# A long convolution and a two-layer block on one core: first x chunk in two loads of 96 rows, its second cast behind two tiles, fewer fillers, last-stage pieces of batch 0 in pairs

## The chip, the cores and the metric

The kernel runs on one core of one Trainium2 chip. The time is device microseconds of that core, from the kernel's start to its end. The profile is one execution of the program, taken by the hardware profiler. Engines: PE is TensorE (matmul; PEld its weight loads), DVE is VectorE, ACT is ScalarE, POOL is GpSimd, SP is SyncE, which here only issues transfers.

## The reference

```python
X = np.fft.rfft(x, axis=1)                      # x: 8 batches, 3008 positions, 256 channels
Y = X * (filt_r + 1j * filt_i)[None, :, :]
y = np.fft.irfft(Y, n=3008, axis=1)
h = y.reshape(24064, 256) @ w_in                # 256 x 2048
s = np.sin(alpha * h)
g = h + s * s / (alpha + 1e-09)
out = g @ w_out                                 # 2048 x 256
```

All inputs and the output are float32; inside, the kernel computes in float16 with float32 accumulation.

## The kernel before

**The transform.** 3008 is 47 x 64, so the transform of each channel is done in four stages of small matrix products per batch: stage 1 over the 47, stage 2 over the 64 with the twiddles in its table (`d_t`), the product with the filter, the inverse of stage 2 (`e_t`), and the last stage (`wi_t`), whose result is written to `y`, which has room for two batches. x is read as 94 rows (`NR`) of 32 x 256 values: row r holds positions 32r to 32r + 31.

**Batch 0 (the head)** has code of its own and stays on the chip between stages, because nothing else can run beside it. Its x is loaded in four chunks. Chunk 0 comes over the hardware queues in float32 into `x32` (lent by `cos_all`): for each half, 80 rows are issued on SP and 14 on ACT, and the table `wf0_t` is issued on ACT between the two. Chunks 1 to 3 are cast on the way by POOL's queue (`load_x`), behind which POOL issues `d_t`, the identity `id16`, the filters and `e_t`. VectorE casts chunk 0 in two halves; then come 16 products of stage 1 (`pa`, L364), evacuated by VectorE (even) and ACT (odd) into `t1_0`. VectorE turns `t1_0` by 32 x 32 blocks (`turn`), copies each filter half to the other partitions (`other_half`), and multiplies (`product_0`). TensorE makes the tables `e1_0` by transposing `d_t` (`pse`, L340), does stage 2 (`pb`, L393) and its inverse (`pc`, L412, through the pool `fps` of two PSUM buffers, evacuated by ACT), and after `turn_back` the last stage.

**Fillers.** `warm_pe(n)` issues n matmuls on zeros (L351) whose result nobody reads, in places where TensorE would stand idle: 19 before stage 1, 2 between groups of stage 1, 5 after it, and 2 and 4 around the first last-stage pieces.

**The last stage** comes in 16 pieces per batch: `last(u)` takes four columns of 94 and one half of the channels. For batch 0 a piece is eight matmuls of 64 columns (`pd`, L258), a buffer of `fps`, and an evacuation into `y`. Without an argument `evac` gives one in three to VectorE and two to ACT, by a counter.

**The dense block** runs over 48 chunks of up to 512 columns of `y`, two batches at a time, in 8 steps each: `hidden` (`ph`, L497, four `hps` buffers; sine on ACT, L500; L501 on VectorE into `v`) twice per step, and `project` of the chunk before (`po`, L513) between. All spectral work of batches 1 to 7, and pieces 4 to 15 of batch 0, is put between dense groups by a list with due times in steps (`put(at, fn, ...)`): `slot(at)` takes what is due, at most one TensorE item at a time unless it is late by more than a step.

```python
for u in range(4, 16):
    put((1,2,3,4,5,6,7,9,16,18,20,22)[u - 4], s0.last, u, pe=True)
...
put(7.5 + 0.3 * i if b == 1 else ..., s.first, i, pe=True)
...
put(12.5 if b == 1 else max(z - 56, 46.5), s.load_t2, g)
```

So batch 1's stage 1 (`first`, `pa`, L183) is due in steps 7.5 to 12; its tiles go to DRAM over SP (`d<-t_h`), come back turned over POOL's queue (`t<-d`, `load_t2`), and its stage 2 (`forward`, `pb`, L203) is due from step 17.5 on. Each engine runs its instructions in the order written; the order in the program is the order of the queues.

Of the kernel before, what the change touches and what calls it, by code (L numbers as in the profile page):

```python
# [18 lines left out]
B, S, C = 8, 3008, 256  # L19
# [3 lines left out]
NR = 2 * N1  # L23
# [39 lines left out]
def kernel(  # L63
# [10 lines left out]
    nc = tc.nc  # L74
# [4 lines left out]
    wf0_dram = nc.inline_tensor(wf0_host, name="wf0_tbl")  # L79
# [38 lines left out]
    cos_all = cpool.tile([128, 4, 512], FP32)  # L118
    y = cpool.tile([128, 2, 2, 32, NR], FP16)
    y_cols = y.rearrange("p a b n r -> p a (b n r)")  # L120
    alpha = y_cols[:, :, 32 * NR:32 * NR + DFF].bitcast(FP32)
    x32 = cos_all.rearrange("p a b -> p (a b)")[0:NR]
    wf0_t = cpool.tile([96, 128], FP16)
    for h in range(2):
        for q, (r0, r1) in ((nc.sync, (0, 80)), (nc.scalar, (80, NR))):
            q.dma_start(out=x32[r0:r1, 4 * C * h:4 * C * h + 4 * C],
                        in_=bass.AP(tensor=x.tensor, offset=x.offset + (32 * r0 + 4 * h) * C,
                                    ap=[[32 * C, r1 - r0], [1, 4 * C]]))
        if h == 0:
            nc.scalar.dma_start(out=wf0_t, in_=wf0_dram.ap())  # L130
    d_t = cpool.tile([128, NS, 128], FP16)
    e_t = cpool.tile([128, NS, 128], FP16)
    wi_t = cpool.tile([NK, NR], FP16)
# [6 lines left out]
    def load_x(b, ch):  # L140
        xt = xpool.tile([NR, 8, C], FP16, name=f"x_{b}_{ch}", tag="x")
        for n0, n in [(0, 8)] if b or ch < 3 else [(0, 4), (4, 4)]:
            ins = nc.gpsimd.dma_start(  # L143
                out=xt[:, n0:n0 + n],
                in_=bass.AP(tensor=x.tensor, offset=x.offset + (b * S + ch * 8 + n0) * C,
                            ap=[[32 * C, NR], [C, n], [1, C]]),
            )
        if b == 0:
            marks["x", ch] = ins
        if b == 1:  # L150
            marks["x1", ch] = ins
            after(ins, marks["w_out"])
        if b > 1:
            after(ins, marks["snake"])
        return xt
# [3 lines left out]
    def evac(dst, src, on_act=None):  # L159
        flip[0] = (flip[0] + 1) % 3  # L160
        if flip[0] if on_act is None else on_act:
            marks["act"] = nc.scalar.copy(out=dst, in_=src)  # L162
        else:
            marks["dve"] = nc.vector.tensor_copy(out=dst, in_=src)  # L164

    class Spectral:
# [82 lines left out]
        def last(self, u, on_act=None):  # L249
# [12 lines left out]
                                     lhsT=t4_h[ch // 2][0:NK, n0 % 16 + i, cb * 128:cb * 128 + 128])  # L262
            evac(y[:, cb, self.b % 2, n0:n0 + 4, :], psv, on_act)

    warm = cpool.tile([128, 1], FP32)
    nc.vector.memset(warm, 0.0)
    nc.scalar.activation(out=warm, in_=warm, func=AFT.Sin)
# [6 lines left out]
    x0 = [xpool.tile([NR, 8, C], FP16, name="x_0_0", tag="x")] + [load_x(0, ch) for ch in range(1, 4)]  # L274
# [17 lines left out]
    def spread_alpha(i):  # L292

        ps = hps.tile([128, 4, 128], FP32, name=f"al_bc_{i}", tag="h")
        for a in range(4):
            for k, part in enumerate(parts):
                nc.tensor.matmul(out=ps[:, a, :], lhsT=one[:, 4 * i + a:4 * i + a + 1].to_broadcast([16, 128]),
                                 rhs=part, start=(k == 0), stop=(k == 2))
        nc.scalar.copy(out=alpha[:, i // 2, 512 * (i % 2):512 * (i % 2) + 512], in_=ps.rearrange("p a b -> p (a b)"))

    for g in range(2):
        gs = slice(12 * g, 12 * g + 12)
        for k, filt in enumerate((filt_r, filt_i)):
            for q in range(2):
                if (g, k, q) == (0, 1, 1):
# [3 lines left out]
                    out=f_t[k][64 * k + 32 * q:64 * k + 32 * q + 32, gs, :],  # L309
                    in_=bass.AP(tensor=filt.tensor, offset=filt.offset + off,  # L310
                                ap=[[N1 * C, 32], [step, 12], [1, C]]))
# [34 lines left out]
    def warm_pe(n):  # L346

        warmed.append(n)
        ps = hps.tile([128, 512], FP32, name=f"warm_{len(warmed)}", tag="h")
        for i in range(n):  # L350
            nc.tensor.matmul(out=ps, lhsT=idle[:, 0:128], rhs=idle[:, 0:512], start=True, stop=True)  # L351
# [3 lines left out]
        gs = slice(12 * g, 12 * g + 12)  # L355
        evac(f_t[k][64 - 64 * k:128 - 64 * k, gs, :], f_t[k][64 * k:64 * k + 64, gs, :], on_act)

    warm_pe(19)
    for h in range(2):
        evac(x0[0].rearrange("p n c -> p (n c)")[:, 4 * C * h:4 * C * h + 4 * C], x32[:, 4 * C * h:4 * C * h + 4 * C], False)  # L360
    for i in range(16):
        own, tag = (fps, "f") if i % 3 == 2 else (hps, "h")
        ps = own.tile([128, 512], FP32, name=f"pa_0_{i}", tag=tag)
        nc.tensor.matmul(out=ps, lhsT=wf0_t[0:NR], rhs=x0[i // 4][:, 2 * (i % 4):2 * (i % 4) + 2, :],  # L364
                         start=True, stop=True)
        evac(t1_0[:, 2 * i:2 * i + 2], ps.rearrange("p (n c k) -> p n c k", n=2, k=2), i % 2)
        if i < 15 and i % 4 == 3:
            warm_pe((2, 2, 2, 5)[i // 4])
    spread_alpha(0)
    spread_alpha(1)  # L370
    warm_pe((2, 2, 2, 5)[3])

    def turn(dst, src):

# [69 lines left out]
    s0 = Spectral(0)  # L444
# [32 lines left out]
    warm_pe(2)  # L477
    s0.last(0, True)
    s0.last(2, True)
    warm_pe(4)  # L480
    s0.last(1, True)
    s0.last(3, False)

# [62 lines left out]
    def put(at, fn, *args, pe=False):  # L546
        pending.append((at, len(pending), pe, fn, args))
# [9 lines left out]

    for i in range(2):
        put(13 + i, negate, i)
    for u in range(4, 16):  # L560
        put((1,2,3,4,5,6,7,9,16,18,20,22)[u - 4], s0.last, u, pe=True)
    for b in range(1, B):
        s = s1 if b == 1 else Spectral(b)
        z = 48 * b
# [87 lines left out]
```

## Time and profile before

| | us |
|---|---|
| four runs | 794.33, 794.27, 794.33, 793.78 |
| median | 794.3 |
| profiled execution, whole | 793.05 |
| its span, first to last instruction | 791.3 |
| PE busy in the span | 779.0 |
| DVE, ACT, POOL busy | 656.5, 617.4, 77.5 |

TensorE is busy for 98% of the span; a busy time here includes the fillers. Most lines of the profile name the program's line, the engine, and what is written and read (`pd<-wi_t,t_h`); a wait is put down to what came last. The head reaches to about 38 us, where the first dense group starts; batch 0's pieces 4 to 11 run from 39.6 to 56, and batch 1's stage 1 from 50 to 65.

### The profile page before, as it was taken

Reading aid. Unit: us, or ns where it says so; the run is one execution under the profiler, and the core shown is the slowest. Engines: PE = TensorE matmul, PEld = TensorE weight load, DVE = VectorE, ACT = ScalarE, POOL = GpSimd, SP = SyncE. Lnnn points to the kernel's source line nnn. Section 1 sums busy time; section 2 is a strip of 40 time slices with the busy share of each in tenths; the row PEclk is TensorE's granted clock in tenths of the full one; section 3 lists DMA queues with packets and bytes.
Section 4 is the critical chain, followed back from the end, with each engine's and each line's share of the span. In section 5 each row is a group of like instructions: output and inputs, shape, how many; then the busy total and the mean of one; then the engine's idle time right before and its main releaser. Section 6 shows DMA issues by size and latency. Waiting matters only on the chain.

```text
span 791.3 us, 16750 instructions
## 1 busy us (share of the span) xinstructions
PE 779.0 (98%) x5865; PEld 536.8 (68%) x5865; DVE 656.5 (83%) x1170; ACT 617.4 (78%) x1210; POOL 77.5 (10%) x119
## 2 busy tenths in 40 slices
PE   8999999999999999999999999999999999999997
PEld 4755666666667766776666766777666776766665
DVE  6877897799878997799978998799987999777773
ACT  5886887888878888788787888788887887777663
POOL 5442000200020000200020000200002000000000
PEclk9999999999999999999999999999999999999999
DMA  9956477755573646654475454845566243421111
GB/s 214 256 107 165 102 157 194 185 108 131 140 204 83 123 111 182 159 117 110 111 209 128 101 107 136 222 90 114 127 169 166 63 99 80 116 60 28 40 41 54
DMA packets 87677, 100.99 MB, mean 128 GB/s; under 512 B 14476, under 2 KB 75932, under 8 KB 87592
## 3 DMA queue, kind: packets, MB, share of 16 engines
q1 hardware_dynamic: 78024, 73.62, 34.3%
q0 software_dynamic: 9296, 26.13, 17.6%
q8 instruction: 46, 0.75, 0.4%
q14 instruction: 39, 0.32, 0.1%
q10 hardware_dynamic: 272, 0.17, 0.1%
HBM read 55.70 MB, written 46.66 MB: 129 GB/s over the span
## 4 chain that ended last, share of the span: by engine, by line
PE 93%; ACT 2%; DMA 2%; DVE 1%; issue 1%; ACTq 0%; POOL 0%; POOLq 0%; DVEq 0%
PE po L513 40%; PE ph L497 39%; PE pa L183 3%; PE pb L203 2%; PE pd L261 2%; PE pc L234 2%; PE pd L258 1%; DVE v L501 1%; ACT cos_all L500 1%; DMA cos_all<-in_x_dram 1%; PE pb L393 1%; PE warm L351 1%; ACT t_h L162 1%; PE pc L412 1%; DMA t<-d 0%
## 5 line engine op out<-in xcount | busy, mean ns | idle before, releaser
L501 DVE SCALAR_TENSOR_TENSOR v<-cos_all,ph 128x512 f16<-128x512 f32 (+1 forms) x768 | 483.0, 671 | 111.7 <-ACT cos_all L500 108.4
L500 ACT ACTIVATE cos_all<-ph 128x512 f32<-128x512 f32 (+1 forms) x768 | 410.9, 591 | 98.6 <-PE ph L497 97.2
L513 PE MATMUL po<-w,v 128*128 128x256 f16 x3008 | 388.7, 272 | 0.0
L497 PE MATMUL ph<-y,w 128*128 128x512 f16 (+1 forms) x1536 | 386.8, 374 | 1.0 <-ACT y L162 0.7
L513 PEld LDWEIGHTS <-v 128*128 128x128 f16 x3008 | 289.3, 98 | 78.2 <-issue 1.8
L497 PEld LDWEIGHTS <-w 128*128 128x128 f16 x1536 | 147.3, 98 | 104.0 <-issue 2.4
L519 ACT COPY o<-po 128x512 f32<-128x512 f32 (+1 forms) x97 | 55.7, 575 | 19.6 <-PE po L513 13.7
L206 ACT CAST xf<-pb 128x512 f16<-128x512 f32 x84 | 49.9, 594 | 16.2 <-PE pb L203 14.1
L195 POOL DMA_DIRECT2D t<-d x56 | 36.3, 667 | 204.8 <-DMA out_dram<-o 129.9
L162 ACT CAST t_h<-pa 96x512 f16<-96x512 f32 x77 | 44.9, 585 | 9.9 <-PE pa L183 9.8
L143 POOL DMA_DIRECT2D x<-in_x_dram x32 | 17.1, 538 | 300.3 <-PE pc L234 160.4
L162 ACT CAST y<-pd 128x376 f16<-128x376 f32 x83 | 39.8, 480 | 7.5 <-PE pd L261 5.3
L261 PEld LDWEIGHTS <-t_h 96*128 96x128 f16 x448 | 31.3, 97 | 18.7 <-DMA t_h<-d 0.6
L183 PE MATMUL pa<-x,wf_t 94*96 94x512 f16 x112 | 42.3, 381 | 1.2 <-DVE t_h L164 0.6
L162 ACT CAST g<-pc 128x512 f16<-128x512 f32 x56 | 33.3, 594 | 7.5 <-PE pc L234 7.2
L224 DVE TENSOR_TENSOR p<-p,xs 128x512 f16<-128x512 f16 x84 | 35.7, 425 | 2.9
L261 PE MATMUL pd<-wi_t,t_h 96*128 96x94 f16 x448 | 37.1, 204 | 0.2 <-ACT cos_all L500 0.2
L223 DVE TENSOR_TENSOR xs<-xs,filt_t 128x512 f16<-128x512 f16 x84 | 35.0, 417 | 0.3 <-DMA xs<-xf 0.3
L217 DVE TENSOR_TENSOR p<-xf,filt_t 128x512 f16<-128x512 f16 x84 | 35.0, 417 | 0.0
L203 PE MATMUL pb<-t,d_t 128*128 128x256 f16 x168 | 32.1, 272 | 1.1 <-DMA t<-d 1.0
L234 PE MATMUL pc<-p,e_t 128*128 128x256 f16 x168 | 32.1, 273 | 0.0
L164 DVE CAST y<-pd 128x376 f16<-128x376 f32 x45 | 24.4, 542 | 0.6 <-PE pd L258 0.5
(63 smaller groups left out, 259.4 us busy)
## 6 DMA issues: line engine op xcount, KB each, us to landing
x<-in_x_dram POOLq DMA_DIRECT2D x30, 376.0 KB, 4.9
d<-t_h SPq DMA_DIRECT2D x28, 384.0 KB
t<-d POOLq DMA_DIRECT2D x56, 192.0 KB, 4.8
xs<-xf SPq DMA_DIRECT2D x168, 64.0 KB
d<-g SPq DMA_DIRECT2D x56, 192.0 KB
t_h<-d SPq DMA_DIRECT2D x28, 384.0 KB
out_dram<-o SPq DMA_DIRECT2D x104, 80.0 KB
w_out<-in_moe_w_out_dram SPq DMA_DIRECT2D x1, 2048.0 KB
```

What stands on the lines that cost most here:

```text
L162: marks["act"] = nc.scalar.copy(out=dst, in_=src)
L183: marks["pe"] = nc.tensor.matmul(out=ps[0:NK, :], lhsT=wf_t, rhs=self.x[ch][:, 2 * j:2 * j + 2, :], start=True, stop=True)
L195: nc.gpsimd.dma_start(out=self.t2[g][64 * p:64 * p + 64, :, :], in_=self.d1[a0:a0 + 6, :, :].rearrange("s n c -> n s c"))
L203: nc.tensor.matmul(out=ps[:, i, :], lhsT=d_t[:, s, :], rhs=self.t2[s // 6][:, s % 6, :], start=True, stop=True)
L206: nc.scalar.copy(out=self.xf[u], in_=ps)
L234: nc.tensor.matmul(out=ps[:, i, :], lhsT=e_t[:, 2 * w + i, :], rhs=pt[:, i, :], start=(k == 0), stop=(k == len(pr) - 1))
L261: nc.tensor.matmul(out=psv[:, i, :], rhs=wi_t, start=True, stop=True, lhsT=t4_h[ch // 2][0:NK, n0 % 16 + i, cb * 128:cb * 128 + 128])
L497: nc.tensor.matmul(out=ps[:, 0:n], lhsT=w1[:, cb, jb * 128:jb * 128 + 128], rhs=y_cols[:, cb, c0:c0 + n], start=(cb == 0), stop=(cb == 1))
L500: nc.scalar.activation(out=cs[:, 0:n], in_=ps[:, 0:n], func=AFT.Sin, bias=float(np.pi / 2))
L501: marks["snake"] = nc.vector.scalar_tensor_tensor(out=v[k][:, jb, 0:n], in0=cs[:, 0:n], scalar=-1.0, in1=ps[:, 0:n], op0=ALU.add, op1=ALU. ...
L513: nc.tensor.matmul(out=pso[k][:, t % 2, :], lhsT=v[k][:, jb, 128 * t:128 * t + 128], rhs=w2[:, jb, :], start=(jb == 0), stop=(jb == 15))
L519: nc.scalar.copy(out=o[:, i0:t % 2 + 1, :], in_=pso[k][:, i0:t % 2 + 1, :])
```

## The change

Chunk 0 of x is loaded by two transfers on SP of 96 rows each; the two rows beyond 94 hold values of the next batch and are not read afterwards. The table `wf0_t` becomes the first transfer that ACT issues. The second cast of chunk 0 is written behind stage 1's tiles 0 and 1, with three fillers ahead of it on TensorE. The filler counts change as shown. Pieces 4 to 15 of batch 0 are put as six pairs; of a pair, the first is evacuated by ACT and the second by VectorE. On TensorE the order after batch 1's stage 2 has begun is the same but for the pieces that have been moved ahead: pieces 4 to 11 stand ahead of batch 1's stage 1, 12 to 15 between its stage 1 and its stage 2, where before 11 stood inside its stage 1 and 13, 14 and 15 behind the start of its stage 2.

```diff
-    x32 = cos_all.rearrange("p a b -> p (a b)")[0:NR]
+    x32 = cos_all.rearrange("p a b -> p (a b)")[0:96]
     wf0_t = cpool.tile([96, 128], FP16)
     for h in range(2):
-        for q, (r0, r1) in ((nc.sync, (0, 80)), (nc.scalar, (80, NR))):
-            q.dma_start(out=x32[r0:r1, 4 * C * h:4 * C * h + 4 * C],
-                        in_=bass.AP(tensor=x.tensor, offset=x.offset + (32 * r0 + 4 * h) * C,
-                                    ap=[[32 * C, r1 - r0], [1, 4 * C]]))
-        if h == 0:
-            nc.scalar.dma_start(out=wf0_t, in_=wf0_dram.ap())
+        nc.sync.dma_start(out=x32[:, 4 * C * h:4 * C * h + 4 * C],
+                          in_=bass.AP(tensor=x.tensor, offset=x.offset + 4 * h * C, ap=[[32 * C, 96], [1, 4 * C]]))
+    nc.scalar.dma_start(out=wf0_t, in_=wf0_dram.ap())
...
+        def last_two(self, u):
+            self.last(u, True)
+            self.last(u + 1, False)
...
-    warm_pe(19)
-    for h in range(2):
-        evac(x0[0].rearrange("p n c -> p (n c)")[:, 4 * C * h:4 * C * h + 4 * C], x32[:, 4 * C * h:4 * C * h + 4 * C], False)
+    warm_pe(10)
+    def cast_x0(h):
+
+        cs = slice(4 * C * h, 4 * C * h + 4 * C)
+        evac(x0[0].rearrange("p n c -> p (n c)")[:, cs], x32[0:NR, cs], False)
+
+    cast_x0(0)
     for i in range(16):
...
+        if i == 1:
+            warm_pe(3)
+            cast_x0(1)
         if i < 15 and i % 4 == 3:
-            warm_pe((2, 2, 2, 5)[i // 4])
+            warm_pe((2, 2, 2, 1)[i // 4])
     spread_alpha(0)
     spread_alpha(1)
-    warm_pe((2, 2, 2, 5)[3])
+    warm_pe((2, 2, 2, 1)[3])
...
-    warm_pe(4)
+    warm_pe(1)
     s0.last(1, True)
     s0.last(3, False)
...
-    for u in range(4, 16):
-        put((1,2,3,4,5,6,7,9,16,18,20,22)[u - 4], s0.last, u, pe=True)
+    for u in range(4, 16, 2):
+        put((1,2.5,4,6,14,16)[u // 2 - 2], s0.last_two, u, pe=True)
```

## The prediction

> **What bounds the kernel now.** I read the page first, then TensorE's waits, then the chain that ended last, stage by stage, and beside it the timeline of VectorE in the head.
>
> ```profile
> span 791.3 us, 16750 instructions
> PE 779.0 (98%) x5865; PEld 536.8 (68%) x5865; DVE 656.5 (83%) x1170; ACT 617.4 (78%) x1210; POOL 77.5 (10%) x119
> PEclk9999999999999999999999999999999999999999
> ```
>
> TensorE is busy for all but 12 us of the span, at full clock. So an edit pays in two ways only: less time on TensorE, or one of its few waits gone. The waits (who waited for whom, total, times, longest):
>
> ```profile
> PE pa L364 <- DVE x L164: 1.1, 1, 1.1
> PE pb L203 <- DMA t<-d: 1.0, 1, 1.0
> ...
> PE pa L183 <- DVE t_h L164: 0.6, 1, 0.6
> ```
>
> The first is in the head, which the change rebuilds; the second is near 75 us, between batch 1's stage 1 and its stage 2. The chain in the head (start, length, what):
>
> ```profile
> 1.78 6.31 DMA cos_all<-in_x_dram
> ...
> 8.18 0.70 DVE x L164
> ...
> 8.93 0.59 PE pa L364 x2
> ...
> 14.85 1.19 PE warm L351 x5
> 16.04 1.01 PE pse L340 x32
> ```
>
> The first x chunk's second half holds everything: its 14-row load, third on ACT's queue, lands at 8.1. But TensorE is not what carries the head on from there. VectorE's timeline is:
>
> ```profile
> 8.79 5.30 DVE L164 CAST t<-pa 128x512 f16<-128x512 f32 x8
> 14.26 2.37 DVE L375 STREAM_TRANSPOSE t_h<-t 128x1024 uint32<-128x1024 uint32 x2 [0.17 <-ACT t L162]
> 24.21 0.95 DVE L164 COPY filt_t<-filt_t 64x3072 f16<-64x3072 f16 x1
> 25.31 2.97 SPq L427 DMA_DIRECT2D w_in<-in_moe_w_in_dram  x6
> 25.92 0.96 DVE L164 COPY filt_t<-filt_t 64x3072 f16<-64x3072 f16 x1
> ```
>
> Eight evacuations end to end, then transposes, copies and products with hardly a gap until 31 us. The w_in loads at 25.31 wait for the last filter load, so that line shows when it lands: the copy at 25.92 can come at most 0.6 earlier. Later in the chain:
>
> ```profile
> 33.87 1.08 PE pd L258 x16
> 35.92 1.15 PE pd L258 x16
> 41.25 0.66 PE pd L258 x8
> 41.91 0.97 PE ph L497 x4
> 66.57 3.28 DMA d<-t_h
> 71.12 3.62 DMA t<-d
> 75.25 0.86 PE ph L497 x4
> 76.11 0.61 PE pd L258 x8
> 76.72 0.98 PE po L513 x8
> ```
>
> A last-stage piece (8 narrow matmuls) costs 0.61 to 0.66 alone; two in a row cost 1.08 to 1.15. The dense group behind a piece takes 0.97 or 0.98, where it takes 0.86 or 0.87 elsewhere.
>
> **The change part by part.**
>
> *Loads of x.* Two SP loads of 96 rows replace two of 80 on SP and two of 14 on ACT; ACT loses two issues (0.66 and 0.43 us), so the wf load is issued at about 0.75 and not 1.43. Rows 94 and 95 add 2%. By the trace's landing records the two SP halves land near 4.95 and 6.4, the wf table at 6.7, ACT's second half at 8.1. For the 96-row half I bound the landing by 6.4 (the 80-row row, nothing added) and 8.1 (nothing gained). [...] By the rows, what was late was one small load behind two others on its own queue, while SP's own half was there 1.7 sooner; a fifth more rows on SP adds a few tenths. I take 7.0, the nearer row. The later issues of POOL are untouched, and the DMA row of the page stands at 9 or more through the head, so the x chunks 1 to 3, tables and filters land as before.
>
> *Second cast behind two tiles.* VectorE now takes tile 0's evacuation (0.66) ahead of the cast (0.70). First cast 5.2 to 5.9, tiles 0 and 1 at 6.0 (before 7.25, where the 19 fillers ended), evacuation to 7.1, second cast to 7.8, tile 2 at 7.85 instead of 8.93: 1.1 earlier. Queued behind the cast are all other evacuations on VectorE. With x chunk 1 landing at 8.5 and the last piece of chunk 3 at 11.8 (issue near 3.0 plus the 8.8 that the trace gives), the last tile runs at 11.9, stage 1 is evacuated at 13.2 and not 14.23, and the transposes start 1.0 earlier.
>
> Then the stall moves. The identity table lands at 15.1 (issue 4.03 plus 11.1), so the `pse` transposes gain 0.8 at most of the 16.04. The copies of the filters at 24.21 and 25.92 meet their loads: gain 0.5 there. From 28 on TensorE and ACT alternate through two PSUM buffers (the evacuation of each `pc` ahead of the next but one), and ACT, 0.75 ahead by then, brings that chain forward by 0.7. Ends for the head are 0.2 (the filter copies rule, and a bit more is lost) and 1.0 (stage 1's whole gain is kept); I take **0.7**.
>
> *Fillers.* 19 become 10 plus 3; 5 and 4 become 1 each. Eight run at half rate (0.43 us) and end at 4.9, so ten end at 5.3, then 0.7 idle. Where TensorE waits for VectorE anyway they cost nothing; their loss costs something only through the clock. [...] By the trace the price is 0: a gap of 1.08 and a 3.4 us stretch (7.05 to 10.45) with only 2.32 busy kept clock 1.00. The longest new idle is 1.3 (13.9 to 15.2). [...] I take 0.
>
> *Pairs.* Twelve single pieces of batch 0 become six pairs, one evacuated by ACT, one by VectorE; that is nearly the split of before. A single with what it adds to the group behind costs 0.65 + 0.11 = 0.76 among the first eight (0.62 + 0.11 = 0.73 among the last four); a pair 1.11 + 0.11 = 1.22. Early: 8 x 0.76 - 4 x 1.22 = 1.2. Late: 4 x 0.73 - 2 x 1.22 = 0.5. But from 45.7 to 51 the chain runs over ACT (sines, four w_out scalings, evacuations), whose work stays the same. So chunk 0 ends about where it did, with piece 11 done inside it; what stays is that piece's absence from chunk 1, and of 1.2 I take **0.7** (0 to 1.2). Late: **0.5**. Each pair fills both stage PSUM buffers, so the next stage 1 tile waits for ACT's and VectorE's copy in queue order; two dense groups lie between, and I add nothing.
>
> *Where the late pairs stand.* Pieces 13, 14 and 15 used to come after `pb_0`, the product that waits 1.0 us for batch 1's reload; now all stand ahead of it. The write and reload (66.57 to 74.74) start from batch 1's last stage 1 tile, and TensorE's work from there to `pb_0` grows from 8.7 by 2 x 1.22 - 0.73 = 1.7, against a path of 9.5. The wait is covered with 0.9 to spare: **1.0**.
>
> Sum: 0.7 + 0.7 + 0.5 + 1.0 = 2.9. The profiled execution took 793.05 (span 791.3 and 1.75 around it), 1.25 below the median of the four runs; it would take 790.2. The same 2.9 off the median of 794.3 gives 791.4. After 75 us the orders are the same and TensorE is busy throughout, so I see nothing that gives the gain back; I round to 791.5.
>
> **The rivals.**
>
> *Covered gains.* The 96-row half lands near 8, or the filter copies hold the head, and ACT takes all of the early pairs' gain. Only the covered reload and the late pairs are left: 1.0 + 0.5, so 792.8. For it: the ACT stretch of the chain; DMA engines full in the head. Against: SP's own half at 6.4.
>
> *The clock gate closes in the head, and it ends slower.* The place is 5.3 to 15.2, with idle stretches of 0.7, 0.7 and 1.3 us and few fillers. TensorE at half rate costs about 0.5 us for each us of its work on the path: sixteen tiles 3.4 more, the alpha spread 1.4, `pse` and `pb` 2.4, together 7.2, of which idle time takes 2.5. So 4.7 is lost against 2.9 won: 796.1. It decides from about 6 us at half clock. Against: the 3.4 us stretches of before that are only two thirds busy at full clock.
>
> *The change does less than it says:* tile 0's evacuation holds the second cast past the time that its data is there. With the landing at 6.4 this costs 0.7 of a gain that the filter copies cap anyway; it is inside the range of the forecast.
>
> **How the numbers follow.** A change of 0.2% (1.6 us) is about what a measurement of this kernel can tell from none: faster is below 792.7, slower above 795.9. Forecast 0.64 (its own range 790.2 to 792.7), covered gains 0.20 (792.2 to 794.3, a quarter of it below 792.7), clock 0.10, something unlisted on the slow side 0.03, more gain than summed (chunk 1's waits of 0.6 and 0.4 going too) 0.03. Faster 0.64 + 0.05 + 0.03, less a little for the forecast's edge: 0.70; same 0.17; slower 0.13. The range runs from 790.2 to 794.3; it leaves out the clock case and about 0.05 below.
>
> **What would show it.** Right: tile 2 (`pa`, third) near 7.85; stage 1's last evacuation near 13.2; `ph_0` 0.7 earlier than 36.98; pairs as groups of 16 at 1.1; no wait of `pb` on the reload; PEclk still 9 everywhere. Wrong: a clock digit below 9 in the first slices; the second cast waiting for its load until 8; a wait of stage 1 on an evacuation where pairs hold the buffers; or a new wait after 80 us as long as the one removed.

## The result, and the profile after

| | median us (executions) | ratio to the kernel before, 95% interval |
|---|---|---|
| before | 794.33 (50) | 1 |
| changed | 793.28 (32) | 0.9988 (0.9983 to 0.9993) |

The change makes the kernel 0.12% faster: more than the interval, less than the 0.2% that the prediction called a difference, and a third of the 2.9 us that the sum gave. The profiled execution took 793.69 us. From its page:

```profile
span 791.9 us, 16719 instructions
...
PEclk9899999999999999999999999999999999999999
```

The 8 in the last line is new: in the second slice (20 to 40 us) TensorE was not at full clock. A shorter closing of the clock in the first slice, shown below, does not change its digit: with 3.41 us of 19.8 at half clock the mean is still 0.91. TensorE's waits now:

```profile
PE pse L341 <- DMA id<-id: 1.0, 1, 1.0
PE pd L258 <- DMA t_h<-d: 0.8, 1, 0.8
...
PE pa L369 <- DVE x L161: 0.5, 1, 0.5
```

The wait of `pb` on its reload is gone, as forecast, and so is half of the first one. But `pd` of batch 1 now waits for a transfer, where before only its weight load did, for 0.6:

```profile
PEld L261 <- DMA t_h<-d: 0.6, 1, 0.6
```

The chain shows both losses:

```profile
38.85 1.82 PE ph L505 x4
40.67 1.16 PE pd L255 x16
...
67.93 1.11 PE pd L255 x13
...
76.43 0.22 PE pb L200 x2
...
122.29 4.85 DMA d<-g
...
127.21 3.94 DMA t_h<-d
...
131.20 0.34 PE pd L258 x4
```

Four hidden products take 1.82 at 38.85, where they took 0.97: half clock. The pairs are there at 1.1 each, and `pb` (76.43) no longer waits. At 131 the first last-stage piece of batch 1 waits for its write and reload.

To see where the gain is won and lost, I compare the start of the same matmul in both traces. From `pb_4` on the orders are equal, so matmuls can be matched from the end:

| place (time before) | changed is ahead by, us |
|---|---|
| first hidden product (36.98) | 0.52 |
| third hidden product (38.6) | -0.18 |
| batch 1's first stage 1 tile (49.9) | -2.19 (with piece 11 already done) |
| 88.5 | 0.77 |
| 127 | 0.43 |
| 131.5, and then constant to 785 | -0.18 |

After 131 us the matmuls of the two traces run in step to 0.02 us: on TensorE everything is decided before. What comes behind the start of the last matmul took 5.79 us and not 5.34; over all traces here it takes 5.0 to 6.0. This execution is 0.4 over the changed kernel's median, and that of the kernel before, with which every trace below is compared too, is 1.3 under its own (793.05 against 794.33). So a gain read from two traces can be smaller than the one that the medians show, and what the kernel before did in its one trace need not be its rule.

### The profile page after: what moved, and what is told of

The parts are those of the page before. It is cut to its first block, busy times and chain, and to the rows that moved or that the text cites. A ratio compares the mean times of both kernels' runs of the same rounds, so it can differ in the third digit from the quotient of the medians.

```text
span 791.9 us, 16719 instructions
## 1 busy us (share of the span) xinstructions
PE 778.0 (98%) x5852; PEld 536.8 (68%) x5852; DVE 657.7 (83%) x1171; ACT 616.9 (78%) x1209; POOL 78.1 (10%) x119
## 4 chain that ended last, share of the span: by engine, by line
PE 89%; DMA 3%; DVE 3%; ACT 2%; issue 1%; SPq 0%; POOL 0%; ACTq 0%; POOLq 0%
PE ph L505 39%; PE po L521 39%; PE pa L180 3%; PE pd L258 2%; PE pb L200 2%; PE pc L231 2%; DVE v L509 1%; DMA id<-id 1%; PE pd L255 1%; ACT cos_all L508 1%; DMA xs<-xf 1%; DMA d<-g 1%; PE pb L401 1%; DVE t_h L383 1%; ACT t_h L159 1%
## 5 line engine op out<-in xcount | busy, mean ns | idle before, releaser
L203 ACT CAST xf<-pb 128x512 f16<-128x512 f32 x84 | 49.9, 594 | 15.1 <-PE pb L200 12.7
L180 PE MATMUL pa<-x,wf_t 94*96 94x512 f16 x112 | 42.2, 381 | 1.1 <-DVE t_h L161 0.6
L159 ACT CAST g<-pc 128x512 f16<-128x512 f32 x56 | 33.3, 594 | 7.5 <-PE pc L231 7.2
```

What stands on the lines that cost most here:

```text
L180: marks["pe"] = nc.tensor.matmul(out=ps[0:NK, :], lhsT=wf_t, rhs=self.x[ch][:, 2 * j:2 * j + 2, :], start=True, stop=True)
L203: nc.scalar.copy(out=self.xf[u], in_=ps)
```

## The experiments

**The two groups of fillers.** The clock by stretches of 3.41 us in the changed kernel (columns: stretch, its length, busy us and count of PE, PEld, DVE, ACT and POOL, granted clock, DMA share, GB/s), set where the trace's clock record changes:

```profile
11.46:14.88 3.42, 2.42 (x28) 1.66 (x28) 3.15 (x4) 2.48 (x4) 0.90 (x2) 1.00 1.19 261
14.88:18.29 3.41, 3.24 (x44) 2.90 (x43) 3.11 (x4) 2.14 (x3) 2.62 (x4) 0.50 1.17 221
...
25.12:28.53 3.41, 2.64 (x37) 2.21 (x35) 3.28 (x5) 3.41 (x8) 0.00 (x0) 1.00 0.72 183
...
31.94:35.36 3.42, 2.93 (x38) 2.05 (x35) 3.42 (x3) 2.23 (x5) 3.42 (x3) 1.00 1.06 352
35.36:38.77 3.41, 3.30 (x21) 1.57 (x21) 1.62 (x3) 1.16 (x3) 3.41 (x3) 0.50 1.10 350
38.77:42.19 3.42, 3.42 (x23) 1.65 (x23) 2.68 (x6) 2.18 (x4) 1.09 (x2) 0.50 0.23 72
```

The clock was halved from 14.9 to 18.3 and from 35.4 to 42.2 (granted clock 0.50 in these three rows; the expectations below call it a closing of the gate, at 15.1 and 35.6; their zero is 0.2 off). Each time the stretch just before is one from which the change took fillers: 5 to 1 after stage 1, 4 to 1 between the first last-stage pieces. So I put both groups back.

```diff
-            warm_pe((2, 2, 2, 1)[i // 4])
+            warm_pe((2, 2, 2, 5)[i // 4])
...
-    warm_pe((2, 2, 2, 1)[3])
+    warm_pe((2, 2, 2, 5)[3])
...
-    warm_pe(1)
+    warm_pe(4)
     s0.last(1, True)
```

> The changed kernel with the two removed groups of fillers back (5 after stage 1, 4 between the first last-stage pieces), all else of the change kept. Clock theory: the gate closed because these fillers went, at 15.1 for 3.4 us and at 35.6 for 6.8 us. With them the clock is 1.00 from 5 us on, four hidden products take 0.97 and not 1.82, the first project starts at about 51.0 instead of 53.5, and the median falls by 1.0 to 2.5 us below the changed kernel's 793.3. Rival, absorption: whatever is won in the first 80 us is held by the reload before batch 1's last stage (t_h<-d, landing at 131.15 in both traces), so the clock is full and the time is within 0.3 us of the changed kernel.

Measured: 791.48 us (5 executions), ratio 0.9959 (0.9946 to 0.9972). The clock stayed full to 789 us in the profiled execution. Its chain:

```profile
37.61 0.97 PE ph L505 x4
...
124.95 4.18 DMA t_h<-d
129.18 0.34 PE pd L258 x4
```

Four hidden products are back at 0.97. Of the kernel before it is ahead by 1.07 at the first hidden product, 2.98 at 88 us and 2.85 at 127, and then by 1.84 from 132 to the end. The two groups are worth 1.8 us by the medians and 2.3 by the ratios, so the rival falls as the main cause; but in this execution 1.0 of the gain is lost at the reload that the last two lines show. The intervals of this kernel and of the changed one do not overlap.

Then each group alone. Only the 4:

> The changed kernel with only the 4 fillers before the second pair of last-stage pieces back; the group after stage 1 stays at 1. Clock theory: the closing at 35.6 goes, the one near 15 stays. The closing near 15 hits work that VectorE covers (pb began at 16.97 against 17.05 before), so this one edit brings nearly all that both groups bring: within 0.4 us of the kernel with both back. Rival: the closing near 15 is worth as much as the other (about 1 us each), since TensorE's transposes took 1.92 and not 1.01.

Measured: 792.00 us (6), ratio 0.9965 (0.9953 to 0.9978), 0.5 over the kernel with both, in overlapping intervals. But in the profiled execution the gate closed at another place, from 23.5 to 26.9, and neither near 15 nor near 35, and it was ahead by only 0.96 at 88 us. That is 2.0 less than with both groups, and a wait stands just ahead of the closing:

```profile
PE pc L420 <- DMA e_t<-e_tbl: 1.1, 1, 1.1
```

The inverse table landed late: the first `pc` ran at 22.48, with both groups at 20.59. So 1.9 of the 2.0 were lost before the gate closed, and the closing itself cost about 0.1. The next expectation puts all of it down to the closing, which is wrong. Only the 5:

> The changed kernel with only the 5 fillers after stage 1 back; the group between the first last-stage pieces stays at 1. Clock theory: the closing near 15 goes, the one near 35.6 stays and with it most of the loss, since the stretch behind it is dense work that nothing covers: a median near 792.8, within 0.6 us of the changed kernel, mean clock near 0.996. Rival: what costs is the closing near 15 (with 4 fillers only, one execution lost 2 us to a closing at 23.7), and the median falls to 791.5 to 792.0.

Measured: 792.45 us (9), ratio 0.9974 (0.9965 to 0.9983), mean granted clock 0.995. The clock was halved from 35.3 to 42.1, just as in the changed kernel, and nowhere else in the head. The time lies between the two forecasts: the clock theory is right on the place, and the 5 fillers are worth something too, 0.8 us by the medians and 1.1 by the ratios. How they win it is not shown: at the first hidden product this trace is ahead of the kernel before by 0.64 and that of the changed kernel by 0.52. The two groups share the 1.8 us, and these intervals do not divide it further.

The kernel before with the fillers cut and nothing else changed (5 to 1, 4 to 1):

> The kernel before with the two groups of fillers cut (5 to 1, 4 to 1) and nothing else changed. Clock theory: the gate closes near 35 also here, and the time rises by 1 to 2.5 us over the kernel before. Rival: the closing needs the earlier loads of the change, which open gaps at 14 and 34; without them the clock stays at 1.00 and the time is within 0.4 us of the kernel before.

Measured: 795.78 us (11) beside 794.78 of the kernel before on that chip; ratio 1.0008 (0.9999 to 1.0017), so the time alone does not settle it. The clock does: all eleven executions have a mean of 0.995 to 0.997, and only 16 of 62 of the kernel before are at 0.997 or below. The windows and the chain of the profiled one:

```profile
35.36:38.77 3.41, 3.11 (x20) 1.45 (x20) 1.58 (x4) 1.07 (x2) 3.41 (x3) 0.50 1.06 335
```

```profile
39.10 1.82 PE ph L497 x4
```

The gate closes near 35 without the earlier loads, too, and this execution was 1.56 us behind the profiled one of before at 88 us and 2.68 at its last matmul. The rival (the closing needs the gaps that the loads open) falls for the second closing. The first one, near 15, did not occur here, so for that one the rival may stand; it did not occur either in two executions that have the earlier loads and 1 filler there (only the 4 back, and the later pieces with 1 and 1 below).

**The pairs and the loads by themselves.** All pairs on the kernel before (`last_two` and its six due times, nothing else):

> The kernel before with the pieces 4 to 15 in pairs and nothing else of the change; loads, casts and fillers as before. Forecast by the sum of the prediction: 0.7 + 0.5 + 1.0 = 2.2 us less, pb's wait on the reload near 75 gone. Rival, absorption by the reload of batch 1's last stage: the difference to the kernel before is 1.5 to 2.2 at 90 us and under 0.5 after 131 us.

Measured: 791.96 us (6), ratio 0.9971 (0.9960 to 0.9982), 2.3 us less by the ratio. The profiled execution was ahead by 1.57 at 88 us, 1.05 at 127 and behind by 0.28 from 132 on, with a wait of 1.5 for the reload (its time, 793.59, is the longest of the six; the others took 791.86 to 792.28). So the 2.2 of the sum is there in the median, and the absorption in this one execution. Clock full to 792 us. Then one half each. Pieces 12 to 15 only:

```diff
-    for u in range(4, 16):
-        put((1,2,3,4,5,6,7,9,16,18,20,22)[u - 4], s0.last, u, pe=True)
+    for u in range(4, 12):
+        put((1,2,3,4,5,6,7,9)[u - 4], s0.last, u, pe=True)
+    for u in range(12, 16, 2):
+        put((14,16)[u // 2 - 6], s0.last_two, u, pe=True)
```

> The kernel before with only pieces 12 to 15 in two pairs (steps 14 and 16); pieces 4 to 11 single as before. Prediction's terms: 0.5 for the pairs and 1.0 for the covered reload, so 1.5 us ahead of the kernel before at 88 us and no wait of pb on the reload; less at the end by what the reload at 131 holds. Rival: piece work ahead of pb makes pb late by as much as the wait it covers, and the gain at 88 us is the 0.5 alone.

Measured: 792.34 us (6), ratio 0.9972 (0.9961 to 0.9984). Ahead by 1.55 at 88 us, with no difference (-0.05) at 65. The chain:

```profile
71.81 1.12 PE pd L258 x15
...
75.65 0.22 PE pb L203 x2
```

No wait of `pb` is left, and 1.55 is the 0.5 + 1.0 of the sum. Of it 0.41 is left after 132 in this execution. Pieces 4 to 11 only (steps 1, 2.5, 4, 6; the last four single):

> The kernel before with only pieces 4 to 11 in four pairs (steps 1, 2.5, 4 and 6); 12 to 15 single as before. Prediction's term: 0.7 us (0 to 1.2) ahead at 66 us, where batch 1's stage 1 ends; the wait of pb on the reload stays near 1.0, and the same gain is left at 88 us. Rival: ACT carries the end of chunk 0, and the gain at 66 us is under 0.2.

Measured: 794.17 us (10), ratio 0.9993 (0.9984 to 1.0002): no difference that the runs resolve. It was 0.29 ahead at the first hidden product, where it does not differ from the kernel before, and 0.68 at the end of batch 1's stage 1, so the pairs brought 0.4. The wait of `pb` then was 1.2 and not 1.0, and at 88 us only 0.43 was left, 0.14 over what the head had given. So the gain ahead of this wait was given to it, and the early pairs alone brought nothing that the runs resolve.

The loads, the second cast and the 10 + 3 fillers on the kernel before, with the groups of 5 and 4 kept:

> The kernel before with the loads, the second cast and the 10 + 3 fillers of the change, the groups of 5 and 4 fillers kept and the pieces single. Clock theory: with 5 and 4 kept the gate stays open, and the loads win by themselves what the prediction gave the head, 0.7 us (0.2 to 1.0), at the start of the first dense group and at 90 us; half or more of it may be held at 131. Rival: the filter copies hold the head (gain at 36 us under 0.4), and the whole gain of the kernel with both filler groups comes from the pairs.

Measured: 794.06 us (12) beside 794.18; ratio 0.9989 (0.9980 to 0.9998), 0.9 us by the ratio and 0.1 by the medians. In the profiled execution, the slowest of the twelve, stage 1 was again 1.0 earlier at its third tile, but the first hidden product was 0.2 late; it was 0.4 behind at 88 us and 1.8 at the last matmul. Its chain and its waits say why:

```profile
11.85 10.62 DMA e_t<-e_tbl
```

```profile
PE pc L420 <- DMA e_t<-e_tbl: 1.2, 1, 1.2
```

The inverse table landed at 22.5, later than `pc` needed it, as with only the 4 fillers back; in the other executions it was in time. So the head's gain depends on how the queued tables land: at the first hidden product it was 0.52 in the changed kernel, 1.07 with both groups back, -0.2 here, and between -0.92 (only the 4 back) and 1.30 over all eight executions with the new loads. (The three with pairs only, whose head is that of before, stand at -0.32 to 0.29.) The forecast's 0.7 is inside that spread. The rival's cap, the filter copies, waited 0.5 us for their loads in the changed kernel and here and not at all with both groups back; here the inverse table with 1.2 is the larger wait.

**The reload at 131 us.** Batch 1's first last-stage piece was put at step 43.5 and TensorE waited 0.8 to 1.5 us for its columns in every execution above but three: in that of before, that with the fillers cut and that with only the 5 back, the piece's weight load waited, for 0.6 to 1.0. The wait does not follow the gain alone: with the loads alone TensorE came there 0.9 later than in the kernel before and still waited 1.1, with the early pairs alone 0.3 earlier, and it waited 1.1. I moved the first two pieces behind a stage 1 tile and one group of `project` (due steps of pieces 0 to 3: 44.5, 45, 45.5, 46.5):

```diff
-            put(z + (u - (4.5 if b == 1 else 6.5) if u < 4 else 2 * u - 9), s.last, u, pe=True)
+            put(z + ((-3.5, -3, -2.5, -1.5)[u] if b == 1 and u < 4 else u - 6.5 if u < 4 else 2 * u - 9), s.last, u, pe=True)
```

First with the fillers of the kernel that has both groups back:

> The kernel with both filler groups back, and the first last-stage piece of batch 1 moved behind one stage 1 tile and one group of project (about 1.1 us of TensorE work), the second behind one more. Absorption theory: what was lost at 131 us (gain 2.85 before, 1.84 after, a wait of 1.2) is only that piece waiting for its reload; with work ahead of it the wait goes, the gain stays near 2.85 to the end, and the median falls by about 1.0 us. Rival: the reload is late for others too, the wait moves to the second piece or to the first dense group of batch 1 (due at once behind them), and the time stays within 0.3 us.

Measured: 791.02 us (5), ratio 0.9945 (0.9933 to 0.9957): 0.5 less than without the move by the medians and 1.1 by the ratios, in overlapping intervals, so between the two forecasts and not resolved. In the profiled execution the gate closed for one stretch, 33.3 to 36.8, in spite of the four fillers, and those four took 1.82 us at half clock and held the pieces behind them; that cost about 1.0. But what was there was kept: 1.62 ahead at 127, 1.63 at 131, 1.77 at the end. With the changed kernel's own fillers (1 and 1):

> The changed kernel, fillers at 1 and 1 as changed, with only batch 1's first two last-stage pieces moved behind a stage 1 tile and a group of project. Absorption theory: of the 0.77 us that the changed kernel was ahead at 88 us, 0.6 was lost to the reload at 131; that stays now: the wait of pd on t_h<-d is gone and the median is 792.3 to 792.8, whatever the clock does. Rival: a late reload is a matter of the one execution and the median stays at 793.3.

Measured: 791.12 us (10), ratio 0.9960 (0.9945 to 0.9976), where the changed kernel had 0.9988. The intervals do not overlap, so the rival falls. The gate closed near 35 as in the changed kernel (34.6 to 41.5), but not near 15. It was ahead by 1.39 at 127, 1.40 at 131 and 1.87 at the end. Of the 2.0 us between the last matmuls of the two profiled executions 0.9 was there at 88 us already and is not from this edit; the rest is the wait, which is gone. That the median fell by more than the 0.5 to 1.0 forecast stays unexplained beyond that. And with three fillers in the second group:

> The kernel with both filler groups and the later pieces, with 3 fillers and not 4 between the first last-stage pieces. In the execution profiled with 4 the gate closed at 33.6 all the same, the four fillers took 1.82 us cold and held the next pieces by 0.8. If fillers at half clock on the path are what is left to win: 0.2 less per cold execution, a median of 790.7 to 791.0. Rival: with 3 the gate closes in more executions, and the median rises to 791.5 or more.

Measured: 790.72 us (5), ratio 0.9955 (0.9942 to 0.9968). The number is the one forecast, but not for its reason: the gate did not close here (clock full to 786 us), so no filler ran cold. (One of the five executions has a mean clock of 0.994; it took 792.74.) The gain was 2.94 at 88 us, 2.47 at 127 and 2.95 at the end. Its chain around the moved piece:

```profile
128.56 0.88 PE po L521 x8
129.44 0.17 PE pd L258 x4
```

`pd` follows `project` at once. More is kept than was there at 127, probably because the wait of the kernel before (0.6 on the weight load) goes as well. This is the best median of all; from the kernels with both groups and 4 fillers, with and without the later pieces (791.02 and 791.48), its interval does not tell it apart. All three beat both kernels.

**The clock in the kernel before.** Its 62 executions beside these experiments are a test that costs nothing: sorted by the mean granted clock that each shows, their medians are

| mean clock | 1.000 | 0.999 | 0.998 | 0.997 | 0.996 |
|---|---|---|---|---|---|
| executions | 10 | 22 | 14 | 11 | 4 |
| median us | 793.93 | 794.15 | 794.95 | 795.47 | 795.68 |

(The one left, at 0.993, took 798.99.) The medians in the table spread over 1.7 us with the clock. The changed kernel's 32 have a mean clock of 0.994; the kernel with both groups back, 0.999. The mean also takes in the end of the program, behind the last matmul: the best kernel's profiled execution has 0.998 with a full clock to 786 us, about what one closing of 3.41 us would leave (half of 3.41 in 790 is 0.002). And this is a correlation; that fillers move the clock is shown by the runs above.

## Why the prediction was right or wrong

The range (790.2 to 794.3) holds 793.28, and the direction was right. The likeliest case was not: 791.5 with 0.70 for a gain over 0.2%, and the gain is 0.12%. The result fell where "covered gains" stood (792.2 to 794.3), but not by that mechanism: two prices that the sum did not have took about as much from it as covered gains would have. That the range holds the number is luck. Step by step:

- **Landing of the 96-row half, 7.0 (6.4 to 8.1).** The second cast started at 6.46, straight behind the evacuation and without a wait, so it had landed by then: the end given by SP's own 80-row load. The third tile ran at 7.19, 0.66 earlier than I had it; 0.5 of that comes from the first cast, which started at 4.70 and not at 5.2.
- **The stall moves to the tables.** Right: `pse` waited 1.0 for the identity and ran at 15.05, and the head kept half of stage 1's gain. The 0.7 measured as 0.52 in the changed kernel and -0.92 to 1.30 among the others with these loads.
- **Fillers cost 0.** This step failed. I took a gap of 1.08 and a stretch that was two thirds busy as proof that the clock holds. The stretch of 11.46 to 14.88 was busy for 2.42 of 3.42, with no gap over 1.02, and the clock went; 31.94 to 35.36 was busy for 2.93, and it went; 25.12 to 28.53 was busy for 2.64, and it held. Neither busy time nor gaps sort the stretches that half clock followed from the others (last section). The closings of the changed kernel last 3.41 and 6.83 us, and in the kernel with both groups and the later pieces one came behind a stretch with 0.18 us idle in all. The clock rival had a chance of 0.10, with a loss of 4.7 us; its closing was in the changed kernel's profiled execution, and the medians put its price near 1.8 (2.3 by the ratios).
- **Pairs, late: 0.5, and the covered reload: 1.0.** Right: 1.55 at 88 us alone.
- **Pairs, early: 0.7.** Mis-sized: 0.4 at the end of batch 1's stage 1. That ACT holds more of chunk 0's end than the half that I took off would fit; no run tells.
- **"After 75 us ... I see nothing that gives the gain back."** This step failed as well. Batch 1's last stage reads a reload like the one near 75, and I had read only TensorE's own waits, where before it does not appear. It was there among the waits of the weight loads, 0.6 us of PEld L261 on `t_h<-d`: the transfer was due just as TensorE came. Against the one trace of before, the traces without the move lose 0.4 to 1.3 us there (0.61 in the changed kernel, 1.01 with both groups back), among them some that came no earlier. So a gain meeting the reload is a part of it; how late the reload is in the kernel before's other executions is not known. What is shown is that moving the pieces takes the wait away and, with the changed kernel's fillers, lowers the time clear of noise.

With the clock held the sum came out: 2.98 us at 88 us against 2.9, in part by luck, since the head gave 1.07 for 0.7 and the early pairs 0.3 for 0.7. What it lacked are two prices, 1.8 us by the medians for the clock and, in these two traces, 0.6 to 1.0 for the reload.

## What to carry to other kernels

Idle time of TensorE that "costs nothing" can still cost clock: here two groups of fillers in such time were worth 1.8 us by the medians. Before a filler is cut, look at what else fills the time around it (here the 24 matmuls of the alpha spread, which kept TensorE busy for 1.50 us, where a filler starts every 0.22 us), and check the granted clock of several executions, since one profile can miss a closing: the one of before shows full clock from 4.9 to 789.9 us, while 16 of the 62 executions have a mean of 0.997 or less. A gain is worth what is left behind the next wait on a transfer (here 0.6 and 1.0 us were lost at the reload near 131 us), so look for transfers that arrive just in time (waits of weight loads too) downstream, and move what reads them along with the gain. Match instructions of the two traces from the end: a difference that stays constant shows where it was decided.

## What was not expected of the hardware

The clock was halved after stretches in which TensorE was busy for 2.42 and 2.93 of 3.42 us. Two more stretches speak against both busy time and gaps as the cause. The first, of the kernel with both groups and the later pieces, was followed by half clock; the second, of the loads alone, kept the full clock with less busy time and a gap of 1.17:

```profile
29.93:33.34 3.41, 3.23 (x46) 2.48 (x45) 3.05 (x2) 2.64 (x5) 3.41 (x3) 1.00 0.97 312
```

```profile
20.58:23.99 3.41, 2.24 (x29) 1.96 (x28) 3.11 (x5) 2.91 (x7) 0.00 (x0) 1.00 0.91 192
```

What differs is the work in the array. Take rows times columns of the array times columns streamed as the work of a matmul, and a filler (128 x 128, 512 columns) as the unit: the 24 matmuls of the alpha spread, over 16 rows, are 0.75 together, a last-stage piece of eight over 64 columns is 0.73, and a matmul across an edge is divided by its time. In the changed kernel's trace the clock changes 10.24, 13.65, 30.72 and 37.55 us behind its first change at 4.64, that is at 3, 4, 9 and 11 times 3.41; in that of before there is no change from 4.86 to 789.93. Stretches of 3.41 us laid off from the first change hold:

| stretch, kernel | TensorE busy, us | work, in fillers | clock in the next stretch |
|---|---|---|---|
| 11.47 to 14.88, changed | 2.42 | 3.3 | 0.50 |
| 31.95 to 35.36, changed | 2.93 | 4.9 | 0.50 |
| 29.93 to 33.34, both groups and later pieces | 3.23 | 5.8 | 0.50 |
| 20.07 to 23.48, only the 4 back | 2.31 | 5.9 | 0.50 |
| 40.17 to 43.59, both groups and later pieces | 2.86 | 6.2 | 1.00 |
| 20.58 to 23.99, loads alone | 2.24 | 6.6 | 1.00 |
| 25.12 to 28.53, changed | 2.64 | 8.3 | 1.00 |

In the traces of before and of the changed kernel, up to 780 us, the three stretches that half clock followed hold 3.3, 4.9 and 5.5 fillers' work, and the other 450 at least 6.2; over all 13 traces 11 such stretches hold 3.3 to 5.9, and the other 2934 at least 6.2. No run varied the work at equal busy time, so it is not shown that the work is what lowers the clock, nor that these numbers hold for any other kernel. With both groups back the stretches at the places of the two closings (11.27 to 14.69 and 31.75 to 35.17) hold 7.4 and 8.1, and the clock stayed full.

Why equal programs differ is not shown either. By execution the clock's first change lies between 4.35 and 7.31 us, and in the trace of before the stretches laid off from it hold 6.9 at the least, while one from 31.7 us on would hold 5.3; no run set the time of that first change.

Fillers on the path are not free at half clock either: with both groups and the later pieces four took 1.82 us, where they took 0.97 with both groups alone.
